# Two attention mixers on one core: V kept in one layout with drains of PE, nine exp tiles, another order of jobs on the shared PSUM bank, and a cubic for half of VectorE's exps

## The chip, the cores and the metric

The kernel runs on one core of one Trainium2 chip. The metric is the device time of one execution in microseconds. A core has TensorE (PE: matrix products), VectorE (DVE), ScalarE (ACT: here the exponentials), GpSimd (POOL) and SyncE (SP, which here only issues transfers). Each works through its own list of instructions in order and waits on semaphores for the others.

## The reference

```python
# x: [1, 2048, 512]; 32 heads of width 16; two attentions over the same x
# A: own q for each head, one k and one v shared by all heads
q = (x @ wq).reshape(B, S, H, Dh).transpose(0, 2, 1, 3); k = x @ wk; v = x @ wv
scores = einsum("bhqd,bkd->bhqk", q, k) * Dh ** -0.5
a = einsum("bhqk,bkd->bhqd", softmax(scores), v) -> [S, H*Dh] @ wo
# B: q, k and v for each head, from wqkv
b = the same with its own k and v, @ wo
g = sigmoid((x * gate_w).sum(-1, keepdims=True))
return g * a + (1 - g) * b
```

Weights and x are normal numbers of spread 0.05; A's wq and wk are multiplied by 8. There are 2 x 32 heads x 2048 x 2048 exponentials, 268 million. No row maximum is taken off in the kernel's fast path: the ranges of inputs, q and k are checked at the end, and a flag runs a general path (`_general`) if a limit is broken.

## The kernel before, in words

**Tiling.** Heads are handled in eight groups, in turn of A and of B (`groups`, L197: a0, b0, a1, b1, ...), eight heads each. A group has two halves of 1024 queries and for each half two phases of four heads: 32 phases (`phases`). A phase has 32 quads (`quads`, L200), each a block of 128 keys (`c`, 16 of them) with one of two pairings `w` of key halves and query blocks. A quad is two exp tiles (four heads): 2048 exp tiles of 128 x 1024 elements in all, keys along the partitions.

**Scores** (`products`, L616): eight matmuls of 64 rows by 32 columns fill a tile of two PSUM banks. Two such tiles alternate. ScalarE reads one with Exp into an SBUF tile of `prob_tiles` (L641, in `score`). There are six of these (`PROBS`).

**V products** (`values`, L669): PE multiplies the exps with V, in fp32, and sums over the 32 quads of a phase in PSUM, in the pair of banks `pair[0]`. The upper and the lower 64 key rows (`rows(i)`) sum into different banks. V has a column of ones, so the softmax's denominators come along. With `w` = 1 the key halves are exchanged, so V is held twice, in straight order and with its halves exchanged (`vA[0]`, `vA[1]`, `vB[0]`, `vB[1]`); the second is made by transfers (`swapped`, L213).

**The shared bank pair** `pair[1]` serves everything else on PE: the q, k and v projections (`project`, L422; 31 of 24 jobs each, L210), V's turning (`turned`), the output projections (`o_unit`, L496, six jobs each) and the scores of tiles whose exps VectorE does (`vector_job`, L799). Only one of these uses it at a time (`free["spare"]`, `current`).

**VectorE's exps** (`chain`, L827): a tile of scores goes through seven instructions: a conversion from PSUM (L843), mantissa (L847) and exponent (L851) by bit operations and four steps of Horner's scheme (L856), in six tiles `vec_tiles`. `pick` (L768) chooses a quad from the end of the present or the next phase, `vector_job` starts a chain if at most three of VectorE's tiles wait for their V product and little is left of the chain before.

**Other work.** After a phase the sums go to SBUF (L747), are rearranged by transfers (L565, SP's queue), divided (L572 to L581) and projected (`o_unit`); the results are scaled by the gate (L521) and added to the output in DRAM by GpSimd's queue (L531). q and k are split in two fp16 parts (L445, L448) and laid out for the scores by transfers of SP and POOL (`lay`, L404). GpSimd splits the weights (L226 to L228).

**What sets the order.** The program is written out while the kernel is made: a planner (`_Plan`) holds an estimated time for each engine. `pe_step` (L940) issues the next score tile as soon as its PSUM tile and an exp tile are free, and between two of them takes one job after another while it ends before the next exp is due. It asks, in this order, for V products of ScalarE's tiles (`mine`), for a job of the shared bank (`spare`) and for V products of VectorE's tiles (`other`); near a phase's end `other` comes ahead of `spare`. VectorE's instructions are chosen by rank and due time (`vector`, L107). Constants such as `EXP` (estimated distance of two exps, 904 ns) and `CHAIN` are the planner's.

## Time and profile before

| | |
|---|---|
| device time, median of 3 runs | 1826.82 us (1824.4 to 1826.92) |
| span of the profiled execution, first to last instruction | 1822.2 us |
| instructions | 95700 |
| busy: PE, VectorE, ScalarE, GpSimd | 96%, 73%, 98%, 17% |
| mean granted clock of TensorE | 0.996 |
| exp tiles on ScalarE, on VectorE | 1926, 122 |
| DMA moved | 109.39 MB, mean 60 GB/s |

The profiled execution has no time of its own beside its span; the median of the runs is 4.6 us above it. A row of the profile names the source line, engine, operation, output tile <- input tiles, shape and count; then busy time and mean duration of one; then the engine's idle time before such instructions and what ended it. Matmul rows overlap each other, so their busy time is not work; distances of starts are. A row of stretches gives begin:end and length in us, busy time and count of each engine, then the granted clock, the DMA share and GB/s.

### The profile page before, as it was taken

Reading aid. Unit: us, or ns where it says so; the run is one execution under the profiler, and the core shown is the slowest. Engines: PE = TensorE matmul, PEld = TensorE weight load, DVE = VectorE, ACT = ScalarE, POOL = GpSimd, SP = SyncE. Lnnn points to the kernel's source line nnn. Section 1 sums busy time; section 2 is a strip of 40 time slices with the busy share of each in tenths; the row PEclk is TensorE's granted clock in tenths of the full one; section 3 lists DMA queues with packets and bytes.
Section 4 is the critical chain, followed back from the end, with each engine's and each line's share of the span. In section 5 each row is a group of like instructions: output and inputs, shape, how many; then the busy total and the mean of one; then the engine's idle time right before and its main releaser. Section 6 shows DMA issues by size and latency. Waiting matters only on the chain.

```text
span 1822.2 us, 95700 instructions
## 1 busy us (share of the span) xinstructions
PE 1742.1 (96%) x44697; PEld 844.5 (46%) x44697; DVE 1332.0 (73%) x1507; ACT 1778.7 (98%) x1942; POOL 305.1 (17%) x367
## 2 busy tenths in 40 slices
PE   8999999999999999999999999999999999999896
PEld 5544444444444444444444444444444444444442
DVE  5277656779667597869767569796967676788994
ACT  5999999999999999999999999999999999999995
POOL 2212001202020131231102023133200111012000
PEclk9999999999999999999999999999999999999998
DMA  5121111323121142433212123342312122236111
GB/s 152 36 61 44 46 58 55 90 55 67 32 62 32 39 83 55 75 65 66 44 42 63 32 66 56 67 84 63 64 20 57 44 55 57 42 67 149 36 61 61
DMA packets 64883, 109.39 MB, mean 60 GB/s; under 512 B 14480, under 2 KB 22928, under 8 KB 64480
## 3 DMA queue, kind: packets, MB, share of 16 engines
q0 software_dynamic: 21504, 43.99, 13.6%
q1 hardware_dynamic: 39744, 56.99, 11.4%
q8 instruction: 351, 5.75, 1.3%
q10 hardware_dynamic: 3232, 2.23, 0.4%
q14 instruction: 52, 0.43, 0.1%
HBM read 14.75 MB, written 33.55 MB: 27 GB/s over the span
## 4 chain that ended last, share of the span: by engine, by line
ACT 86%; issue 8%; PE 4%; DVE 1%; DMA 1%; ACTq 0%; POOL 0%; DVEq 0%
ACT prob L641 85%; PE pair L682 1%; PE sc L627 1%; PE pair L301 0%; DVE vec L856 0%; PE pair L1173 0%; DMA prob<-in_A_wv_dram 0%; DVE xT L1295 0%; DMA vec<-in_A_x_dram 0%; DVE xT L515 0%; DMA Qa<-loqa 0%; PE pair L335 0%; DVE dT L572 0%; ACT early L641 0%; PE pair L210 0%
## 5 line engine op out<-in xcount | busy, mean ns | idle before, releaser
L641 ACT ACTIVATE prob<-sc 128x1024 f32<-128x1024 f32 x1905 | 1749.7, 1134 | 3.8 <-PE sc L627 3.2
L682 PE MATMUL pair<-prob,vA 64*32 64x512 f32 (+1 forms) x8048 | 510.4, 566 | 0.0
L682 PE MATMUL pair<-prob,vB 64*32 64x512 f32 (+1 forms) x8016 | 508.4, 569 | 0.0
L856 DVE SCALAR_TENSOR_TENSOR vec<-vec,vec 128x1024 f32<-128x1024 f32 x366 | 445.9, 1242 | 2.8
L627 PE MATMUL sc<-Qb,K 64*32 64x512 f16 x7632 | 395.9, 380 | 37.2 <-ACT prob L641 26.8
L627 PE MATMUL sc<-Qa,kA 64*32 64x512 f16 x7776 | 401.8, 380 | 21.7 <-ACT prob L641 11.6
L627 PEld LDWEIGHTS <-K 64*32 64x32 f16 x8192 | 201.2, 89 | 414.8 <-issue 375.1
L627 PEld LDWEIGHTS <-kA 64*32 64x32 f16 x8192 | 199.8, 89 | 390.2 <-issue 346.6
L843 DVE TENSOR_SCALAR vec<-pair 128x1024 int32<-128x1024 f32 x122 | 148.4, 1216 | 64.5 <-PE pair L627 64.4
L682 PEld LDWEIGHTS pair<-prob,vA 64*32 64x32 f32 x8048 | 155.3, 105 | 20.0 <-issue 1.4
L682 PEld LDWEIGHTS pair<-prob,vB 64*32 64x32 f32 x8016 | 153.5, 105 | 19.0 <-DVE raw L747 0.7
L856 DVE SCALAR_TENSOR_TENSOR vec<-vec 128x1024 f32<-128x1024 f32 x122 | 151.8, 1247 | 0.6
L531 POOL DMA_DIRECT2D out_dram<-sum x48 | 60.6, 1284 | 387.6 <-DVE sum L521 373.0
L572 DVE RECIPROCAL dT<-dT 128x256 f32<-128x256 f32 (+1 forms) x66 | 111.4, 1694 | 18.9 <-DMA dT<-raw 18.6
L747 DVE COPY raw<-pair 128x1024 f32<-128x1024 f32 x31 | 37.9, 1224 | 95.8 <-PE pair L682 95.2
L847 DVE TENSOR_SCALAR vec<-vec 128x1024 int32<-128x1024 int32 x122 | 84.1, 692 | 2.8 <-PE pair L682 1.3
L851 DVE TENSOR_SCALAR vec<-vec 128x1024 int32<-128x1024 int32 x122 | 84.5, 695 | 0.0
L521 DVE TENSOR_SCALAR sum<-pair,gate_up 128x512 f32<-128x512 f32 x112 | 78.6, 740 | 6.3 <-PE pair L210 6.0
L404 POOL DMA_DIRECT2D Qa<-hiqa x31 | 17.3, 558 | 305.6 <-DVE hiqa L445 284.5
L210 PEld LDWEIGHTS <-o 64*32 64x32 f16 x3072 | 50.1, 93 | 39.3 <-ACT o L578 8.1
L404 POOL DMA_DIRECT2D Qb<-hiqb x32 | 18.4, 574 | 293.3 <-DVE o L578 169.1
L210 PE MATMUL pair<-w16ob,o 64*32 64x512 f16 x1488 | 61.1, 384 | 6.0 <-ACT o L578 6.0
(160 smaller groups left out, 1182.7 us busy)
## 6 DMA issues: line engine op xcount, KB each, us to landing
out_dram<-sum POOLq DMA_DIRECT2D x48, 512.0 KB, 5.8
vB<-vB SPq DMA_DIRECT2D x16, 384.0 KB, 4.9
dT<-raw SPq DMA_DIRECT2D x32, 128.0 KB, 3.1
oT<-raw SPq DMA_DIRECT2D x32, 128.0 KB, 3.4
out_dram<-sum SPq DMA_DIRECT2D x8, 512.0 KB, 2.9
xT<-out_dram SPq DMA_DIRECT2D x16, 256.0 KB, 3.3
dT<-raw SPq DMA_DIRECT2D x62, 64.0 KB, 2.2
out_dram<-xT SPq DMA_DIRECT2D x12, 256.0 KB, 2.4
```

Source lines behind the costliest of these rows:

```text
L210: nc.tensor.matmul(outs[n : n + COLS, i], lhs[i][rows(i), n : n + COLS], rhs[i][rows(i)], start=start, stop=stop)
L521: nc.vector.tensor_scalar(state["sum"][:, e], pair[1][:, e], g, None, op0=ALU.mult)
L531: done = plan.on_pool([lambda: nc.gpsimd.dma_start(dst, state["sum"], accum_op=ALU.add)], t, 1300)
L572: nc.vector.reciprocal(d[:, c : c + cut], d[:, c : c + cut])
L627: nc.tensor.matmul(bank[a : a + COLS, hh], k[rows(hh), key : key + COLS], Q[src, gi, half, p][rows(hh), j * BLK : (j + 1) * BLK], start=Tr ...
L641: nc.scalar.activation(probs[u], sc, AF.Exp, scale=SCALE / (UP * UP))
L682: nc.tensor.matmul(pair[0][32 * k : 32 * k + 32, i, cols], v[rows(i)], probs[2 * m + k // 2][rows(i), hh, cols], start=first, stop=last)
L747: nc.vector.tensor_copy(state["raw"], full)
L843: nc.vector.tensor_scalar(tile("p").bitcast(I32), pair[1], SCALE / (UP * UP) / math.log(2) * 2.0 ** 23, None, op0=ALU.mult)
L847: nc.vector.tensor_scalar(tiles["m"].bitcast(I32), tiles["p"].bitcast(I32), 0x7FFFFF, 125 << 23, op0=ALU.bitwise_and, op1=ALU.bitwise_or)
L851: nc.vector.tensor_scalar(tiles["w"].bitcast(I32), tiles["p"].bitcast(I32), 0x7F800000, 0x40000000 | LEAD, op0=ALU.bitwise_and, op1=ALU.bi ...
L856: nc.vector.scalar_tensor_tensor(p, m if i == 3 else p, VEC[i], m if i else w, op0=ALU.add, op1=ALU.mult)
```

## The change

V is held once. The scores keep the keys in place and exchange the query blocks instead (`j = a // ROWS ^ w`), so with `w` = 1 the upper and lower rows of a V product write the other bank of `pair[0]`. A phase's quads come in runs of the same `w` (8, 16 and 8 long), and where the V products change `w` within three score tiles, PE executes a drain first. The memory of the second V gives three more exp tiles. While more than `LEFT` (near a phase's end `LEFT_END`) exp tiles are free, the order of asking is `spare`, `mine`, `other`. VectorE's tiles of B take three instructions, a cubic in factored form; to bound B's scores the check of q_b takes sums of magnitudes over a head by a matmul (`magnitudes`) in place of a plain maximum. `pick` goes by runs, with less lead (`CHAIN` 16000); a tile of VectorE's is summed when its `w` suits the present run or free tiles are few. Transfers that lay out q and k are issued once the tiles they overwrite are no longer needed (`behind`); V's turning waits for the old group's V products.

```diff
-EXP, EXP_ENDS, EXP_AFTER = 904, 1136, 456
+EXP, EXP_ENDS, EXP_AFTER = 916, 1148, 456
-PROBS, VECS = 6, 6
+PROBS, VECS = 9, 6
+LEFT, LEFT_END = 2, 4
+DRAINED, KEPT, SPARED = 180, 2, 2
...
-    vA = [cst.tile([P, NT, DH, 2], F32, name=f"vA{w}") for w in range(2)]
-    vB = [cst.tile([P, NT, 4, 3, DH], F32, name=f"vB{w}") for w in range(2)]
+    vA = cst.tile([P, NT, DH, 2], F32, name="vA")
+    vB = cst.tile([P, NT, 4, 3, DH], F32, name="vB")
...
-    quads = [(ph, c, w) for ph in range(len(phases)) for c in range(NT) for w in range(2)]
+    ORDER = [(c, w ^ h) for h in range(2) for w in range(2) for c in range(8 * h, 8 * h + 8)]
+    FIRST = [(c, 0) for c in (0, 4, 1, 2, 3, 5, 6, 7)] + ORDER[8:]
+    quads = [(ph, c, w) for ph in range(len(phases)) for c, w in (ORDER if ph else FIRST)]
+    runs = [[] for _ in range(3 * len(phases))]
+    for m in range(len(quads)):
+        runs[m // 32 * 3 + (m % 32 >= 8) + (m % 32 >= 24)].append(m)
...
-            swapped(vA[1][:, ts], vA[0][:, ts], queue)
...
+    waiting = []
+    def behind(m, fn):
+        waiting.append((m, fn))
+    def reads():
+        for m, fn in list(waiting):
+            if at[0] >= m and not (half_vec and half_vec[0] // 2 < m):
+                waiting.remove((m, fn))
+                fn(plan.pe)
...
-                plan.vec(lambda: absmax(kind, 2 * gi + half, hilo[0], AX.XY), 1130, 4, end, due=end + 8000)
+                if kind == "q_b":
+                    plan.vec(lambda: magnitudes(2 * gi + half, hilo[0]), 330, 2, end, due=end + 4000, room=lambda: free_vecs)
+                else:
+                    plan.vec(lambda: absmax(kind, 2 * gi + half, hilo[0], AX.XY), 1130, 4, end, due=end + 8000)
...
-                    put(hilo, end)
+                    s = 2 * (2 * gi + (src == "b")) + half
+                    behind(64 * (s - 1) if part == "q" else 256 * gi, lambda t: put(hilo, max(t, end)))
...
+    def magnitudes(n, hi):
+        tile = free_vecs.popleft()
+        mag = tile.rearrange("p a q -> p (a q)")[:, :BLK]
+        nc.vector.tensor_scalar(mag.bitcast(I32), hi.rearrange("p e t -> p (e t)").bitcast(I32), 0x7FFF7FFF, None, op0=ALU.bitwise_and)
+        mag = mag.bitcast(F16).rearrange("p (e t) -> p e t", e=2)
+        def job():
+            for i in range(2):
+                for e in range(2):
+                    nc.tensor.matmul(pair[1][COLS * e : COLS * (e + 1), i], heads16[rows(i)], mag[rows(i), e], start=True, stop=True)
+            free_vecs.append(tile)
+        def finish(t):
+            def top():
+                nc.vector.tensor_reduce(stats[: 2 * COLS, KINDS.index("q_b"), n : n + 1], pair[1][: 2 * COLS], axis=AX.XY, op=ALU.max)
...
-                done = plan.on_sp([lambda: swapped(vB[1][:, ts], vB[0][:, ts], nc.sync)], end, 2 * ISSUE_SP)
...
-        units.append(_Unit(jobs, finish, lambda now: True, lambda: 0, f"turn{gi}{half}"))
+        units.append(_Unit(jobs, finish, lambda now: pv_at[0] >= 8 * gi, lambda: 0, f"turn{gi}{half}"))
...
-                key = c * P + (a + ROWS * w) % P
-                j = a // ROWS
+                key = c * P + a
+                j = a // ROWS ^ w
...
+        if turns(m):
+            nc.tensor.drain()
+            summing[w ^ 1] = -3
...
-                nc.tensor.matmul(pair[0][32 * k : 32 * k + 32, i, cols], v[rows(i)], probs[2 * m + k // 2][rows(i), hh, cols],
+                nc.tensor.matmul(pair[0][32 * k : 32 * k + 32, i ^ w, cols], v[rows(i)], probs[2 * m + k // 2][rows(i), hh, cols],
                                  start=first, stop=last)
+        summing[w] = len(plan.starts)
...
+    def suits(m):
+        rest = [x for x in range(32 * pv_at[0], 32 * pv_at[0] + 32) if x not in vector and x not in added]
+        return not rest or quads[rest[0]][2] == quads[m][2] or len(free_vecs) < SPARED
+    def turns(m):
+        begun = put_in[0] + len(going) > (m in [x for x, _ in going.values()])
+        return begun and summing.get(quads[m][2] ^ 1, -3) + 3 > len(plan.starts)
...
-            can = [m for m, t in pending[pv_at[0]] if (m not in vector) == mine and max(t, v_time(m)) <= now]
+            can = [m for m, t in pending[pv_at[0]] if (m not in vector) == mine and max(t, v_time(m)) <= now and (mine or suits(m))]
...
-        ns = HALF * wide * 2 // BLK
+        ns = HALF * wide * 2 // BLK + (DRAINED if turns(m) else 0)
...
-        need = CHAIN + plan.backlog(3)
...
+        need, left = CHAIN + plan.backlog(3), 0
+        for r in range(at[0] // 32 * 3, min(at[0] // 32 * 3 + 6, len(runs))):
+            found = [m for m in runs[r] if m not in vector and m >= at[0]]
+            left += 2 * len(found)
+            if left * EXP > need and len(found) > KEPT and found[-1] >= at[0] + 2:
+                break
...
+        if source(quads[u // 2][0]) == "b":
+            def first():
+                nc.vector.tensor_scalar(tile("p"), pair[1], CUBE[0] * SCALE / (UP * UP), CUBE[1], op0=ALU.mult, op1=ALU.add)
+            def second():
+                nc.vector.scalar_tensor_tensor(tile("w"), tiles["p"], CUBE[2], tiles["p"], op0=ALU.add, op1=ALU.mult)
+            def third():
+                nc.vector.scalar_tensor_tensor(p, w, CUBE[3], p, op0=ALU.add, op1=ALU.mult)
...
-    CHAIN, MOST, EARLY = 24000, 18, 12
+    CHAIN, EARLY = 16000, 12
...
-        first = (spare, mine, other) if begins and len(free_probs) > 1 else (mine, other, spare) if ending else (mine, spare, other)
+        first = (spare, mine, other) if begins and len(free_probs) > 1 or len(free_probs) > (LEFT_END if ending else LEFT) else (mine, other, spare) if ending else (mine, spare, other)
...
-        nc.vector.tensor_scalar(lim[:, r + k : r + k + 2], highest[:, ix("q_a") : ix("q_b") + 1],
-                                S_MAX / (DH * SCALE), None, op0=ALU.is_le)
+        for src, most in (("q_a", S_MAX / (DH * SCALE)), ("q_b", B_MAX / SCALE)):
...
```

71 lines of the change are left out of this document (44 added, 27 removed).

## The prediction

> **What bounds the kernel now.** I read the page first (busy time, then the chain that ended last), then the rows of the exp line, then stretches of the span.
>
> ```profile
> span 1822.2 us, 95700 instructions
> PE 1742.1 (96%) x44697; PEld 844.5 (46%) x44697; DVE 1332.0 (73%) x1507; ACT 1778.7 (98%) x1942; POOL 305.1 (17%) x367
> ACT 86%; issue 8%; PE 4%; DVE 1%; DMA 1%; ACTq 0%; POOL 0%; DVEq 0%
> L641 ACT ACTIVATE prob<-sc x1905: 1017/1145/1182, 28.1 to 1799.7; 128x1024 f32<-128x1024 f32 x191
> L641 ACT ACTIVATE vec<-sc x10: 1019/1026/1096, 33.7 to 62.9; 128x1024 f32<-128x1024 f32 x10
> L641 ACT ACTIVATE early<-sc x8: 1017/1031/1107, 38.4 to 63.8; 128x1024 f32<-128x1024 f32 x8
> L641 ACT ACTIVATE vB<-sc x3: 1024/1024/1030, 47.5 to 51.9; 128x1024 f32<-128x1024 f32 x3
> 929.74 103.82 ACT L641 ACTIVATE prob<-sc 128x1024 f32<-128x1024 f32 x113
> ```
>
> ScalarE is busy 98% and carries the chain. It does 1905 + 10 + 8 + 3 = 1926 exp tiles, first start 28.1, last 1799.7: 1771.6 us for 1925 distances, 0.920 each. The last row is an undisturbed stretch of 113: with the last one's own 1.15 taken off, (103.82 - 1.15) / 112 = 0.917 us from start to start. So only 1771.6 - 1925 x 0.917 = 6 us are gaps; 28.1 lie before the first exp and 22.5 behind the last start. The time is the number of exps on ScalarE times 0.917 plus about 57. An exp tile moved to VectorE is worth 0.917 us, if PE and VectorE keep up.
>
> [...]
>
> VectorE takes 122 of the 2048 tiles (122 x the five rows below). Is it full, and is PE?
>
> ```profile
> L843 DVE TENSOR_SCALAR vec<-pair 128x1024 int32<-128x1024 f32 x122 | 148.4, 1216 | 64.5 <-PE pair L627 64.4
> L847 DVE TENSOR_SCALAR vec<-vec 128x1024 int32<-128x1024 int32 x122 | 84.1, 692 | 2.8 <-PE pair L682 1.3
> L851 DVE TENSOR_SCALAR vec<-vec 128x1024 int32<-128x1024 int32 x122 | 84.5, 695 | 0.0
> L856 DVE SCALAR_TENSOR_TENSOR vec<-vec 128x1024 f32<-128x1024 f32 x122 | 151.8, 1247 | 0.6
> L856 DVE SCALAR_TENSOR_TENSOR vec<-vec,vec 128x1024 f32<-128x1024 f32 x366 | 445.9, 1242 | 2.8
> 258.00:480.00 222.00, 213.66 (x5463) 101.84 (x5455) 156.77 (x172) 221.84 (x243) 39.23 (x47) 1.00 0.26 64
> 480.00:703.00 223.00, 217.04 (x5632) 104.69 (x5617) 165.05 (x182) 222.77 (x244) 37.21 (x46) 1.00 0.23 53
> 703.00:921.00 218.00, 209.79 (x5392) 101.00 (x5391) 169.03 (x185) 217.84 (x239) 48.16 (x48) 1.00 0.32 61
> 1585.00:1802.00 217.00, 203.66 (x5072) 95.22 (x5056) 179.09 (x211) 215.27 (x235) 19.84 (x22) 1.00 0.30 69
> ```
>
> The last four rows are stretches of one head group each (groups alternate A, B): B's first, A's second, B's second, B's last; behind the length stand busy PE, PE loads, VectorE, ScalarE, GpSimd. VectorE is idle 40 to 65 us in each. The page's 96% for PE overstates it, since pipelined matmuls overlap; so I price PE by distances of starts.
>
> ```profile
> 784.86 0.41 PE L627 MATMUL sc<-Qb,K 64*32 64x512 f16 x8
> 785.08 0.63 PE L210 MATMUL pair<-w16oa,o 64*32 64x512 f16 x16
> 785.63 0.41 PE L627 MATMUL sc<-Qb,K 64*32 64x512 f16 x8
> 785.84 1.05 PE L682 MATMUL pair<-prob,vB 64*32 64x512 f32 x16
> 786.70 0.41 PE L627 MATMUL sc<-Qb,K 64*32 64x512 f16 x8
> ```
>
> A tile's scores take 0.22 (784.86 to 785.08), a product job of eight matmuls 0.22 (0.63 - 0.41), the V product of a pair of tiles (a quad) 0.86 (785.84 to 786.70). Two ScalarE slots last 1.84 and hold 0.22 + 0.43 + 0.22 + 0.86 = 1.73: 94% full, 0.11 idle. The product and exp counts by stage (same four stretches, L210 then L843):
>
> ```profile
> 258.00:480.00 222.00, 45.67 (x1152) 18.70 (x1152) 1.00 0.26 64
> 480.00:703.00 223.00, 49.08 (x1264) 20.48 (x1264) 1.00 0.23 53
> 703.00:921.00 218.00, 41.10 (x1048) 16.82 (x1040) 1.00 0.32 61
> 1585.00:1802.00 217.00, 30.68 (x768) 12.40 (x760) 1.00 0.30 69
> 258.00:480.00 222.00, 17.01 (x14) 1.00 0.26 64
> 480.00:703.00 223.00, 19.48 (x16) 1.00 0.23 53
> 703.00:921.00 218.00, 19.43 (x16) 1.00 0.32 61
> 1585.00:1802.00 217.00, 21.98 (x18) 1.00 0.30 69
> ```
>
> A group has 256 tiles, so 256 x 0.22 + 128 x 0.86 = 166 us of scores and V products, and products of 1152/8 x 0.22 = 32, 35, 29, 21. PE's need is 198, 201, 195, 187 of 222, 223, 218, 217: 86 to 90%. PE has some 20 us left per group, VectorE 40 to 65.
>
> Why does VectorE take no more? Its scores and all projections share one PSUM bank, `pair[1]`:
>
> ```profile
> L210 PE MATMUL pair<-xT,w16vb x192: 376/376/376, 989.1 to 1009.5; 64*32 64x512 f16 x192
> DVE hikb L445 <- PE pair L210: 75.1, 8, 15.9
> DVE hivb L445 <- PE pair L210: 72.4, 8, 15.5
> DVE hiqb L445 <- PE pair L210: 42.6, 8, 15.3
> DVE hiqa L445 <- PE pair L210: 36.9, 7, 7.3
> ```
>
> One projection, 24 jobs of 0.22 or 5.3 us of PE, is spread at two jobs per two slots over 20.4 us, and 31 of them hold the bank a third of the time. Meanwhile VectorE runs dry: 227 us of its idle time ended with a projection's last product.
>
> **The change, part by part.**
>
> Cubic for B's exps. Five kinds of operation in seven instructions, 1.216 + 0.692 + 0.695 + 1.247 + 3 x 1.242 = 7.58 us, become one from PSUM and two in SBUF: 1.216 + 2 x 1.242 = 3.70. In B's second group VectorE has 169 - 16 x 7.58 = 48 us of other work, so it could do (0.9 x 209 - 48) / 3.70 = 38 tiles instead of 16. A's stay at 7.58. For this, q_b's check costs a mask and a job of the shared bank more: eight times about 0.36 (half of the 692 row) and 0.22 of PE, 5 us over the span, hidden in VectorE's idle time.
>
> Shared banks' products first, nine tiles. While more than two tiles are free, jobs of the bank go ahead of V products: a slot then holds three jobs rather than one, until the spare tiles are used up. A projection shrinks from 20.4 to about 12 us (estimate: some four slots of three jobs, the rest at one or two). No PE work is saved; the V products put off return as a debt, and PE's room decides.
>
> V held once. Sixteen transfers of vB (the row below) and four of vA go from SP's and POOL's queues, off the path: V is ready most of a group before its use, which hides them. Without that cover the price would be the 4.9 us of landing.
>
> ```profile
> vB<-vB SPq DMA_DIRECT2D x16, 384.0 KB, 4.9
> K<-lokb SPq DMA_DIRECT2D x32, 64.0 KB, 3.2
> ```
>
> Delayed stores of Q and K (`behind`): sixteen DMAs per projection, alternately on SP and POOL, are issued later, but still 64 quads (over 110 us) before use for Q, 128 for K; landing takes 3.2. V's turn waits until the old group's V products are done; behind it wait only the hi/lo buffers, so the next projection. Cost nothing; cover gone, a projection starts some us late with 110 us to spare. The waits move out of the in-order queues into the program's order.
>
> Drains. Two changes of row halves per phase make 64; a quad of VectorE's out of the run's order adds up to two, so with about 91 quads of VectorE 64 to 246. I take 128, 16 a group. No drain is in this trace. What it exposes is the tail behind the last start of a group: 0.41 - 0.22 = 0.19; with nothing overlapped, all 0.41. I take 0.2, nearest the tail, 3 us per group; ends 64 x 0.19 = 12 to 246 x 0.41 = 101 us of PE in all. Queued behind a drain are the next V product and then the scores that the next exp waits for; in the full pattern they have about 0.1 to 0.2 us of slack, so I put nothing on ScalarE. [...]
>
> The sum. How full can PE get? 94% is the present full pattern; nine tiles let a job fall where the 0.11 was idle. I take 95%; ends 92% (about now) and 98%.
> - B's second and third: (195 + 3) / 0.95 = 208 us, 227 slots, 29 tiles for VectorE instead of 16: +12.6 each (VectorE 75% busy).
> - B's first: 201 / 0.95 = 212, 231 slots, 25 instead of 14: +11.
> - B's last: 190 / 0.95 = 200, 218 slots, 38; VectorE at 90%, with 179 - 18 x 7.58 = 43 of other work, does 37 instead of 18: +19.
> - A's second to fourth: 204 / 0.95 = 215, 234 slots would allow 22; VectorE, with 165 - 16 x 7.58 = 44 of other work and still seven instructions a tile, at 87% does 19 instead of 16: +3 each. A's first: none.
>
> That is +55 in B, +9 in A: 64 tiles, 59 us. Gaps, start and end stay at 57: span 1763.5, against 1822.2. The median of the runs shown, 1826.82, is 4.6 above this span (the record gives the profiled execution no other time). **Predicted: 1768 us.** [...]
>
> **Rivals.**
> 1. PE packs no better (92%): B gains 5, 5, 4, 12, A nothing: 26 tiles, 24 us, 1803. For it: every full stretch shows the same 0.11 idle. Against: B's last group is only 86% full.
> 2. Tiles are held, not computed faster: at most four of VectorE's may wait for their V product, which now comes last in order and only when its half suits. With one batch per phase, 32 x 4 = 128 tiles: 6 us, 1821. Against: the stretches are 8 and 16 quads long, so there are two chances a phase, and lack of tiles overrides the fit.
> 3. Both engines pack better (PE 98%, VectorE 92%): B +20, +20, +18, +19, A +4 each: 93 tiles, 85 us, 1742.
> 4. Slower: each drain stalls ScalarE, because the scores behind it come later than their slack. With 246 drains at the whole 0.41, 101 us of idle exps: 1827 - 59 + 101 = 1869. It decides from 59 / 246 = 0.24 us of stall per drain. For it: scores run only just ahead, since both score banks are in use. Against: the tail row is 0.19, and the order gives a slot with a drain less work.
> 5. The change doesn't do what it says: if q times k of B passed the new limit, the general path would run behind the fast one and the time would multiply. With weights and x of spread 0.05, scores are hundredths; under 1%.
>
> **How the numbers follow.** Main 0.58, PE at 92% 0.17, held tiles 0.10, better packing 0.07, slower 0.08. The main case's own range is 1750 to 1790. The range of 8 in 10 reaches past case 1 and to case 3: 1740 to 1815. A measurement tells 0.2% (3.7 us; the three runs spread 2.5) from no change. Faster: 0.58 + 0.17 + 0.07 + half of the held case 0.05 = 0.87; same 0.05; slower 0.08.
>
> **What would show it.** Right: some 1862 exps on ScalarE, 0.917 apart in undisturbed stretches; about 186 chains on VectorE, two thirds in B at three instructions; projections of 10 to 14 us; PE's need about 95% of each group. Wrong: idle time of ScalarE behind score matmuls near drains beyond the present 6 us (rival 4); counts near 130 with VectorE idle and the bank free (rival 2); projections still 20 us long. If the distance of exps moves from 0.917 by 0.01, 19 us change hands that no step above has.

## The result and the profile after

The change makes the kernel slower: 1869.56 us (median of 4 runs, 1864.53 to 1875.38) against 1825.61 for the kernel before in the same runs, a ratio of 1.0247 (95% interval 1.0233 to 1.0260). 1768 was predicted, and "faster". In the kernel after, the exps stand on L689, the scores on L675, the V products on L734, the jobs of the shared bank on L220, the drain on L724, VectorE's cubic on L946, L949 and L953, and its long chain from L908 on.

The page of the kernel after, its span and busy time:

```profile
span 1867.5 us, 115071 instructions
PE 1767.6 (95%) x54505; PEld 1039.6 (56%) x54505; DVE 1214.0 (65%) x1348; ACT 1763.4 (94%) x1908; POOL 280.7 (15%) x363
```

VectorE does less than before (65% against 73%) and ScalarE is busy 94% instead of 98%, while PE executes 54505 + 54505 = 109,010 matmuls and weight loads instead of 89,394. VectorE and ScalarE have less to do, PE more, and the span is 45.3 us longer: something makes them wait. First the exps (rows of the exp line; the last two numbers of a time are first and last start):

```profile
L689 ACT ACTIVATE prob<-sc x1875: 1014/1081/1194, 27.3 to 1844.2; 128x1024 f32<-128x1024 f32 x188
L689 ACT ACTIVATE vec<-sc x9: 1024/1031/1077, 37.2 to 65.9; 128x1024 f32<-128x1024 f32 x9
```

With five into `early` and three into `vB` these are 1892 exps, 34 fewer than before. I took all 1891 distances of their starts. Those below 930 ns have a mean of 909.8 ns (before: 914.9), and what the longer ones have above this mean I call **excess**. Then the 45.3 us are: 34 exps fewer, -31.1; a distance shorter by 5.1 ns, -9.6 (why it is shorter, no run here shows); excess 96.6 instead of 10.4, +86.2; ahead of the first and behind the last start 50.6 as before, 0. So the exps saved were worth what I said, there were half as many, and 86 us of waiting came that no term of the sum had.

Whom does ScalarE wait for, and whom does that one wait for? The waits of the kernel after (total us, times, longest us), and ahead of them the row of before that answers to the second:

```profile
PEld pair L682 <- issue: 2.7, 8, 0.7
```

```profile
ACT prob L689 <- PE sc L675: 62.5, 70, 3.2
PEld pair L734 <- issue: 97.6, 164, 3.4
PE pair L734 <- issue: 24.2, 24, 2.9
PEld pair L734 <- DVE raw L811: 8.7, 11, 1.9
```

ScalarE waits for score matmuls, and PE, ahead of V products, for "issue": nothing that the profile shows, neither a semaphore nor a transfer. (A larger row of this kind, weight loads ahead of scores, stands in both kernels and is not the loss: 721.7 us before, 357.8 after, some 0.27 each.) The last row, a wait for VectorE's copy of a phase's sums, had 0.7 us before. One place of such an "issue", PE's timeline of the kernel after from 758 us on:

```profile
761.31 0.43 PE L675 MATMUL sc<-Qb,K 64*32 64x512 f16 x8
...
762.06 0.41 PE L675 MATMUL sc<-Qb,K 64*32 64x512 f16 x8
762.27 0.62 PE L734 MATMUL pair<-prob,vB 64*32 64x256 f32 x14
765.78 0.40 PE L734 MATMUL pair<-prob,vB 64*32 64x256 f32 x1 [2.89 <-issue]
```

PE is in the middle of a V product of 16 matmuls: 14 are through, the last two have nothing to wait for, and one of them starts three microseconds later. Between the first and the last exp PE has 26 pauses of over 1 us, and before it had none.

**Where they stand.** I numbered all of PE's instructions in the trace in their order (matmuls, loads, drains, semaphore instructions). 21 of the 26 stand ahead of an instruction whose number leaves 193 when divided by 256, and no other remainder comes twice; the other five wait for VectorE (the copy L811 of a phase's sums, or the low part of q, L468). PE's program comes in blocks of 256 instructions, as the queue that carries it shows (packets, MB, share):

```profile
q8 instruction: 428, 7.01, 1.6%
```

109,010 / 256 = 426, and the 7.01 MB in 428 packets are 16.4 KB each. I read a pause at the end of a block as a block that hasn't arrived yet.

The trace has the times of these packets too. In the pause above one landed at 764.42, and PE went on at 765.78, 1.36 us later. With blocks and packets counted from the first, PE goes on behind each of the 21 pauses 1.22 to 1.54 us after the landing of the packet whose number is one below that of the block end. Where a block ends without a gap, that packet landed 1.9 us ahead (median; 3.2 in the kernel before), and at none of 423 block ends less than 1.18. So it is its block that PE waits for in these pauses, and nowhere does it start on one sooner than 1.18 us after the landing.

**Why PE has more instructions.** The planner cuts a V product in two halves of 256 columns where the room until the next score doesn't hold the whole. A half takes as many matmuls and loads as a whole: 904 products cut in two are 28,928 instructions more in b_halves, 32 each. The rows of the V products of before (min/median/max ns):

```profile
L682 PE MATMUL pair<-prob,vA x8048: 373/589/614, 35.3 to 1584.3; 64*32 64x512 f32 x175, 64*32 64x256 f32 x22
L682 PE MATMUL pair<-prob,vB x8016: 373/589/613, 258.6 to 1801.4; 64*32 64x512 f32 x179, 64*32 64x256 f32 x17
```

and of after:

```profile
L734 PE MATMUL pair<-prob,vA x13896: 372/376/1057, 35.9 to 1632.6; 64*32 64x256 f32 x175, 64*32 64x512 f32 x24
L734 PE MATMUL pair<-prob,vB x11616: 372/376/614, 268.6 to 1845.9; 64*32 64x256 f32 x144, 64*32 64x512 f32 x53
```

The usual V product was 512 columns wide and is now 256: with the jobs of the shared bank first, the room that is left is rarely enough for a whole one. The rate of instructions follows. Stretches of 10 us of the kernel after (behind the length busy time and count of PE, its loads, VectorE, ScalarE, GpSimd; then granted clock, DMA share, GB/s):

```profile
740.00:750.00 10.00, 9.92 (x320) 5.60 (x312) 5.62 (x12) 10.00 (x12) 0.87 (x1) 1.00 0.37 57
750.00:760.00 10.00, 8.58 (x273) 4.84 (x257) 1.92 (x3) 8.63 (x10) 3.65 (x3) 1.00 0.74 109
760.00:770.00 10.00, 7.11 (x239) 4.38 (x244) 1.41 (x2) 6.76 (x9) 0.00 (x0) 1.00 0.33 54
```

320 + 312 instructions in 10 us are 63 per us, a block in 4.05 us; the kernel before has 49 per us over its span, a block in 5.2. In the first row the blocks come in time, in the other two they don't. What differs is the DMA share ahead of the two pauses, that of 756.94 and that of 762.52; the 4 us ahead of each (the share adds up the times of the packets and can be over 1: 1.10 in the first):

```profile
752.94:756.95 4.01, 4.01 (x150) 2.43 (x135) 0.52 (x1) 4.01 (x6) 0.00 (x0) 1.00 1.10 185
758.52:762.53 4.01, 3.79 (x128) 2.38 (x127) 0.00 (x0) 3.38 (x4) 0.82 (x1) 1.00 0.73 97
```

For 416 block ends of the trace I took the DMA share of the 4 us ahead: where it was below 0.6, none of 348 had a pause over 1 us; from 0.6 on, 20 of 68 had one. The program's queue is one of those whose packets the page counts on the 16 DMA engines, beside the kernel's transfers: 1.6% of their time for the program, 13.2%, 9.6% and 0.4% for the three queues of transfers.

### The profile page after: what moved, and what is told of

It is laid out like the page before. It is cut to its first block, busy times and chain, and to the rows that moved or that the text cites. A ratio compares the mean times of both kernels' runs of the same rounds, so it can differ in the third digit from the quotient of the medians.

```text
span 1867.5 us, 115071 instructions
## 1 busy us (share of the span) xinstructions
PE 1767.6 (95%) x54505; PEld 1039.6 (56%) x54505; DVE 1214.0 (65%) x1348; ACT 1763.4 (94%) x1908; POOL 280.7 (15%) x363
## 2 busy tenths in 40 slices
DMA packets 63454, 104.08 MB, mean 56 GB/s; under 512 B 14160, under 2 KB 22480, under 8 KB 62976
## 3 DMA queue, kind: packets, MB, share of 16 engines
q0 software_dynamic: 21440, 43.86, 13.2%
q8 instruction: 428, 7.01, 1.6%
## 5 line engine op out<-in xcount | busy, mean ns | idle before, releaser
L689 ACT ACTIVATE prob<-sc 128x1024 f32<-128x1024 f32 x1875 | 1738.0, 1085 | 64.9 <-PE sc L675 62.5
L734 PE MATMUL pair<-prob,vA 64*32 64x256 f32 (+1 forms) x13896 | 603.5, 398 | 23.3 <-issue 15.3
L734 PE MATMUL pair<-prob,vB 64*32 64x256 f32 (+1 forms) x11616 | 554.7, 434 | 13.6 <-issue 7.0
L675 PE MATMUL sc<-Qa,kA 64*32 64x512 f16 x7760 | 436.1, 381 | 10.1 <-ACT prob L689 4.3
L675 PE MATMUL sc<-Qb,K 64*32 64x512 f16 x7376 | 406.7, 380 | 20.7 <-ACT prob L689 10.9
L734 PEld LDWEIGHTS pair<-prob,vA 64*32 64x32 f32 x13896 | 286.9, 106 | 116.3 <-issue 49.2
L675 PEld LDWEIGHTS <-K 64*32 64x32 f16 x8192 | 194.2, 90 | 273.7 <-issue 218.1
L675 PEld LDWEIGHTS <-kA 64*32 64x32 f16 x8192 | 189.7, 90 | 204.3 <-issue 139.8
L734 PEld LDWEIGHTS pair<-prob,vB 64*32 64x32 f32 x11616 | 236.2, 106 | 79.9 <-issue 32.0
L921 DVE SCALAR_TENSOR_TENSOR vec<-vec,vec 128x1024 f32<-128x1024 f32 x162 | 197.2, 1226 | 2.0
L946 DVE TENSOR_SCALAR vec<-pair 128x1024 f32<-128x1024 f32 x102 | 123.2, 1208 | 46.9 <-PE pair L675 44.4
L953 DVE SCALAR_TENSOR_TENSOR vec<-vec,vec 128x1024 f32<-128x1024 f32 x102 | 124.9, 1229 | 0.8
L949 DVE SCALAR_TENSOR_TENSOR vec<-vec 128x1024 f32<-128x1024 f32 x102 | 123.8, 1223 | 0.8
L908 DVE TENSOR_SCALAR vec<-pair 128x1024 int32<-128x1024 f32 x54 | 66.0, 1222 | 74.7 <-PE pair L675 72.6
L220 PEld LDWEIGHTS <-o 64*32 64x32 f16 x3072 | 56.5, 93 | 40.0 <-ACT o L626 8.8
L811 DVE COPY raw<-pair 128x1024 f32<-128x1024 f32 x31 | 37.8, 1220 | 52.5 <-PE pair L734 52.5
L734 PE MATMUL pair<-vec,vB 64*32 64x256 f32 (+1 forms) x1568 | 66.4, 386 | 3.1 <-issue 1.9
L921 DVE SCALAR_TENSOR_TENSOR vec<-vec 128x1024 f32<-128x1024 f32 x54 | 66.4, 1230 | 1.0
```

Source lines behind the costliest of these rows:

```text
L220: nc.tensor.matmul(outs[n : n + COLS, i], lhs[i][rows(i), n : n + COLS], rhs[i][rows(i)], start=start, stop=stop)
L675: nc.tensor.matmul(bank[a : a + COLS, hh], k[rows(hh), key : key + COLS], Q[src, gi, half, p][rows(hh), j * BLK : (j + 1) * BLK], start=Tr ...
L689: nc.scalar.activation(probs[u], sc, AF.Exp, scale=SCALE / (UP * UP))
L734: nc.tensor.matmul(pair[0][32 * k : 32 * k + 32, i ^ w, cols], v[rows(i)], probs[2 * m + k // 2][rows(i), hh, cols], start=first, stop=last)
L908: nc.vector.tensor_scalar(tile("p").bitcast(I32), pair[1], SCALE / (UP * UP) / math.log(2) * 2.0 ** 23, None, op0=ALU.mult)
L921: nc.vector.scalar_tensor_tensor(p, m if i == 3 else p, VEC[i], m if i else w, op0=ALU.add, op1=ALU.mult)
```

## The experiments

**Theory 1**, formed from the trace of after: PE can't be supplied with that many instructions; the halves are the cause. **Theory 2** is the rival from the prediction: the drains stall ScalarE. A third reading is that the new order of jobs alone is late. The first three runs put one part alone into the kernel before; the fourth takes halves out of the kernel after by one constant, and drains and exps move along with it. The table has all runs, each with its ratio to runs of the kernel before made beside it (medians 1824.7 to 1825.6); the last three columns split the excess of the exps by what lies in the interval or shortly ahead of it: a gap of over 0.2 us in PE's starts at the end of a block, a drain (or both, shown behind the plus sign), or neither.

| kernel | us | ratio to before, 95% | exps | PE instructions | block end | drain + both | neither |
|---|---|---|---|---|---|---|---|
| before | 1825.61 | 1 | 1926 | 89,394 | 3.5 | 0 | 6.9 |
| after | 1869.56 | 1.0247, 1.0233 to 1.0260 | 1892 | 109,010 | 46.4 | 12.7 + 9.2 | 28.2 |
| b_halves | 1879.84 | 1.0282, 1.0257 to 1.0308 | 1926 | 118,322 | 58.7 | 0 | 15.8 |
| b_drains | 1846.48 | 1.0113, 1.0095 to 1.0131 | 1926 | 89,394 | 2.8 | 30.1 + 4.9 | 5.3 |
| b_cubic | 1817.10 | 0.9947, 0.9928 to 0.9966 | 1912 | 89,650 | 7.3 | 0 | 12.3 |
| a_tight574 | 1824.40 | 0.9995, 0.9985 to 1.0004 | 1874 | 96,850 | 20.8 | 16.4 + 1.9 | 28.0 |
| b_quarters | 2762.43 | one run | 1926 | 183,858 | 921.8 | 0 | 26.2 |
| b_prodhalves | 1870.53 | 1.0238, 1.0216 to 1.0261 | 1926 | 107,442 | 47.0 | 0 | 15.8 |
| a_left35 | 1833.26 | 1.0050, 1.0033 to 1.0067 | 1908 | 97,650 | 17.3 | 7.3 + 1.3 | 15.0 |
| a_nocubic | 1886.18 | 1.0330, 1.0313 to 1.0348 | 1916 | 107,346 | 34.7 | 14.8 + 11.0 | 33.8 |
| a_drain2 | 1881.78 | 1.0324, 1.0296 to 1.0352 | 1892 | 109,010 | 50.9 | 16.6 + 13.5 | 25.8 |
| a_left35_fewdrains | 1833.27 | 1.0047, 1.0033 to 1.0060 | 1902 | 98,322 | 19.8 | 1.0 + 0 | 21.0 |
| b_copies | 1853.15 | 1.0153, 1.0119 to 1.0188 | 1926 | 89,394 | 31.4 | 0 | 9.7 |
| b_halves_copies | 2019.84 | 1.1079, 1.1058 to 1.1101 | 1926 | 118,322 | 184.2 | 0 | 23.2 |

### Halves alone, in the kernel before

```diff
-        wide = BLK if n == 0 and plan.scant() and room + TIGHT - SLACK >= 2 * HALF else BLK // 2
+        wide = BLK // 2
```

> The kernel before with one edit: every V product is cut in two halves of 256 columns, where before 904 of the 1024 went at full width. Same arithmetic, same order, same 1926 exps on ScalarE, no drain; PE gets some 904 x 32 = 28900 instructions more (from 89400 to about 118300). Theory 1 (PE is fed too slowly: it stops once it needs more than some 64 instructions a us, as in the 4 us before the long stops of the changed kernel): 118300 / 64 = 1848 us for the instructions alone and with head and tail 1860 to 1910, with many stops of PE over 1 us that wait for nothing. Theory 2 (the drains cost the time) and theory 3 (PE's arithmetic is full): within 5 us of before, 1821 to 1831, since the columns streamed are the same and there is no drain.

Measured: +54.7 us by the medians (51.5 by the ratio) with nothing else changed: no drains, no cubic, the old order, V twice. From its page and its waits:

```profile
span 1878.6 us, 124628 instructions
PE 1774.7 (94%) x59161; PEld 1097.6 (58%) x59161; DVE 1333.4 (71%) x1507; ACT 1794.1 (96%) x1942; POOL 300.3 (16%) x367
```

```profile
PEld pair L682 <- issue: 36.3, 62, 2.0
ACT prob L641 <- PE sc L627: 40.6, 65, 2.3
```

The same two rows as in the kernel after stand up. All 19 pauses over 1 us between the first and the last exp lie at the same remainder, 193.

### Drains alone, in the kernel before

```diff
+        if put_in[0] in (8, 16, 24) and cols.start == 0:
+            nc.tensor.drain()
         for k in range(4):
```

> The kernel before with 96 drains of PE added, ahead of the V products of the 9th, 17th and 25th quad of each phase; nothing else. Theory 1: PE has room for them, at most +8 us (1826 to 1834), for 96 x the tail of 0.19 us is 18 us of PE work of which most is idle time now. Theory 2 (drains stall ScalarE): the 0.41 us of a whole group or more each, +40 us, 1865 or above.

Measured: +21.3 us, between the two expectations. The kernel has 91 of the 96 drains, 0.23 us each: at the other five places a second half comes, and the edit asks for a first. The drain's row and the wait (PEldq is the queue of PE's instructions):

```profile
L676 PEldq DRAIN  x91: 435/470/955, 54.4 to 1809.9; - x91
```

```profile
PEld pair L684 <- issue: 41.9, 98, 0.6
```

A drain holds PE for 0.47 us, and about half of it reaches ScalarE, so a drain isn't free, but 91 of them aren't the 44 us either. The excess at drains is larger than the cost, 30.1 to 35.0 us: the distance of the other exps is 909.7 ns instead of 914.9, and that gives 10 us back. No pause over 1 us came with them.

### The cubic alone, in the kernel before

```diff
+        if groups[phases[quads[u // 2][0]][0]][0] == "b":
+            # first, second, third: one tensor_scalar from PSUM, two scalar_tensor_tensor, as in the change
...
+            return
         a = plan.vec(convert, 1130, 1, t + TO_VEC, (), spared, room=lambda: free_vecs)
```

The check of q_b isn't widened with it, so nothing bounds B's scores for the cubic; the condition under which the last output tiles are loaded early is eased as in the change.

> The kernel before with only the cubic for VectorE's tiles of B (three instructions instead of seven), and with the outputs of the last group let be loaded while that group's own projections wait, as the changed kernel does; V twice, six tiles, the old order and the old range check stay (the check does not bound B's scores for the cubic). The order has 1912 exps on ScalarE instead of 1926, so 14 x 0.917 = 13 us less: 1813, if the cubic's gain is real and PE can follow. If the gain of a freed VectorE is eaten elsewhere (a rival: PE or the shared bank gives no more), 1822 to 1830.

Measured: 1817.10 us, below both kernels, by half a percent of before (ratio 0.9947). A row of VectorE:

```profile
L882 DVE TENSOR_SCALAR vec<-pair 128x1024 f32<-128x1024 f32 x90 | 109.6, 1218 | 47.3 <-PE pair L628 47.3
```

90 tiles by the cubic and 46 by the long chain, 136 instead of 122: 14 exps fewer, 12.8 us, less 9.2 us of new excess in the profiled execution (whose 1819.47 us is the slowest of its four runs). VectorE was 73% busy before and is 61% busy now, and takes only 14 tiles more: with the chain less than half as long for B, something other than VectorE's time limits most of the number. Which, the run doesn't show.

### Fewer halves, in the kernel after

`TIGHT` is how far past its due time a whole V product may end.

```diff
-SLACK, TIGHT, URGENT = 404, 404, 300
+SLACK, TIGHT, URGENT = 404, 574, 300
```

> The changed kernel with one constant changed: a V product of full width may run 170 ns past the time at which the next scores are due (TIGHT 574 instead of 404). The order then has 673 V products at full width and 702 in halves, instead of 293 and 1462: about 12000 PE instructions fewer (near 96900), 77 drains instead of 96 and 1874 exps on ScalarE instead of 1892. Theory 1: the stops go; 28 + 1874 x 0.91 + 23 and 10 to 30 us of gaps: 1770 to 1795. Theory 2: 77 of 96 drains remain, so about 80% of the excess stays: 1835 to 1855. Theory 3 (PE's arithmetic is full): more exps go to VectorE, PE's arithmetic is the same, so no better than 1860.

Measured: 1824.40 (10 runs), 45 us faster than the kernel after by one number of the planner, but 29 to 54 above what I expected. From its page:

```profile
span 1821.9 us, 102877 instructions
PE 1734.3 (95%) x48425; PEld 927.6 (51%) x48425; DVE 1300.3 (71%) x1426; ACT 1750.6 (96%) x1890; POOL 287.1 (16%) x363
```

12,160 instructions fewer, excess at block ends 46 to 21 us, and 18 exps fewer (16 us), I take it since PE has time for more of VectorE's scores. What I had missed is the rest, 46 us of excess at drains (18) and in 241 small gaps (28), 0.1 us at a time, in which neither a block end nor a drain lies. That the order of jobs itself comes late there is my reading; no run shows it.

### How many instructions per us PE can get

```diff
-        wide = BLK if n == 0 and plan.scant() and room + TIGHT - SLACK >= 2 * HALF else BLK // 2
+        wide = BLK // 4
```

> The kernel before with every V product cut in four pieces of 128 columns: same columns streamed, same 1926 exps on ScalarE, no drain, PE instructions from 89400 to about 183900. Theory 1 (PE is fed at some 64 instructions a us at most): 183900 / 64 = 2870 us, and the mean rate over the span tells the ceiling. Rival (short matmuls just cost a fixed time more each on PE itself): b_halves added 28900 instructions and 55 us, 1.9 ns each, so 94500 more would add 180 us: about 2005.

Measured: 2762.43 us, 183,858 instructions in 2760.7 us, 66.6 per us, a little more than the 64 that I had expected. From its page:

```profile
span 2760.7 us, 190171 instructions
PE 1922.1 (70%) x91929; PEld 1537.9 (56%) x91929; DVE 1343.3 (49%) x1507; ACT 1871.7 (68%) x1942; POOL 287.2 (10%) x367
...
q8 instruction: 720, 11.80, 1.8%
...
L641 ACT ACTIVATE prob<-sc 128x1024 f32<-128x1024 f32 x1905 | 1841.5, 1024 | 840.0 <-PE sc L627 833.7
```

No engine is busy throughout, and the kernel runs at the pace of the blocks: 183,858 / 256 = 718, and 720 packets. 603 of its 605 pauses over 1 us between the first and the last exp stand at the remainder 193, and nine in ten of these end 1.23 to 1.55 us after their packet landed. Outside the pauses over 1 us PE starts 102 instructions per us, so it is not the starting of an instruction that limits it.

### More instructions of another kind

Here the V products stay and the fp16 products of the shared bank are cut in two, so that 18,048 instructions come in other places.

```diff
-                nc.tensor.matmul(outs[n : n + COLS, i], lhs[i][rows(i), n : n + COLS], rhs[i][rows(i)],
-                                 start=start, stop=stop)
+                for c in range(0, BLK, BLK // 2):
+                    cols = slice(c, c + BLK // 2)
+                    nc.tensor.matmul(outs[n : n + COLS, i, cols], lhs[i][rows(i), n : n + COLS], rhs[i][rows(i)][:, cols],
+                                     start=start and c == 0, stop=stop and c > 0)
```

> The kernel before with the products of the projections (the jobs of the shared bank, fp16) cut in two halves of 256 columns each; V products stay as they were. PE instructions from 89400 to about 107400, as many as in the changed kernel, but in other places and in another type. Theory 1: during a projection two slots then need 32 + 64 + 32 = 128 instructions in 1.83 us, 70 a us, above the ceiling of 64, so each of 31 projections of 22 us runs some 9% late, and the output projections in part: +40 to +65 us, 1865 to 1890, with stops of PE. Rival (it is something of fp32 V products in halves): 1821 to 1831.

Measured: 1870.53, as expected by theory 1, with 47 us of excess at block ends. So the loss needs neither V nor its banks nor its fp32; what the two edits share is more and narrower instructions of PE, and b_quarters and the packets say that the number is what counts.

### Less of the new order, in the kernel after

```diff
-LEFT, LEFT_END = 2, 4
+LEFT, LEFT_END = 3, 5
```

> The changed kernel with jobs of the shared bank put first only while more than 3 (near a phase's end 5) exp tiles are free instead of 2 and 4. The order then has 648 V products at full width and 752 in halves (before the edit 293 and 1462), 82 drains, 1908 exps on ScalarE. Theory 1 with the price of a drain from b_drains (0.22 us): 28 + 1908 x 0.91 + 18 for drains + 10 to 25 of stops + 23 = 1815 to 1832. Drains as the main cause: 82 of 96 remain, so above 1850.

Measured: 1833.26, a microsecond above the expected range. Shared jobs go first only while more than three tiles are free; more V products find room as a whole (97,650 instructions), and the excess falls at block ends (46 to 17 us), near drains and in the small gaps. 16 exps more go back to ScalarE (15 us). Halves come from asking the shared bank first.

### Without the cubic, in the kernel after

```diff
-        if source(quads[u // 2][0]) == "b":
+        if False:
```

> The changed kernel without the cubic: VectorE's tiles of B take the seven instructions again; all else stays (the order puts 1916 exps on ScalarE instead of 1892, 345 V products at full width and 1358 in halves, 93 drains). If the cubic gives inside the change what it gave alone (0.917 us for each exp moved), 24 x 0.92 = +22 us: 1885 to 1897. If its gain is lost in a PE that is fed too slowly, the time hardly moves: 1860 to 1875.

Measured: 1886.18, in the expected range: 24 tiles go back from VectorE to ScalarE, and the cubic is worth about 15 us within the change by the ratios (1.0330 - 1.0247 = 0.0083 of 1825), 17.6 by the medians, each against its own runs of before, somewhat less than the 22 of its exps.

### Each drain twice, in the kernel after

```diff
         if turns(m):
             nc.tensor.drain()
+            nc.tensor.drain()
```

> The changed kernel with each of its 96 drains doubled (two in a row), order and all else the same. If a drain costs because PE has to run empty and fill again, the second finds it empty: 0 to +5 us, 1865 to 1875. If each drain costs the 0.22 us of b_drains whatever stands ahead of it (a fixed cost of the instruction), +21 us: 1887 to 1895.

Measured: 1881.78, 12 us above the kernel after, between the two expectations. The drain's row in the kernel after, and the rows of the first and the second of each pair in this one:

```profile
L724 PEldq DRAIN  x96: 457/578/1470, 56.4 to 1834.4; - x96
```

```profile
L724 PEldq DRAIN  x96: 432/616/1462, 56.2 to 1845.1; - x96
...
L725 PEldq DRAIN  x96: 13/13/248, 57.2 to 1845.7; - x96
```

A second drain finds PE empty and takes 13 ns, so the edit doesn't double what I meant to double. The excess grows by 10 us, 8 of them at drains, more than the 1.2 us of the added rows, and why is open. For the price of a drain the run says little.

### Fewer drains

```diff
-LEFT, LEFT_END = 2, 4
-DRAINED, KEPT, SPARED = 180, 2, 2
+LEFT, LEFT_END = 3, 5
+DRAINED, KEPT, SPARED = 400, 2, 0
```

> The kernel of a_left35 (jobs of the shared bank first only above 3 or 5 free tiles) with a V product of VectorE's tiles never let through out of its run (SPARED 0) and a drain reckoned at 400 ns instead of 180 by the order: 40 drains instead of 82, 1902 exps on ScalarE instead of 1908, about as many V products in halves (some 21 more jobs of 32 instructions), and an end some 6 us longer by the order. At 0.22 us a drain: -9 for drains, -5 for exps, +10 for the later end and gaps that the order itself leaves: 1824 to 1832 against a_left35's 1833. If the drains hold most of what is left of the excess (41 us there), below 1820; if drains cost nothing, 1833 to 1840.

Measured: 1833.27 (9 runs), the same as with 82 drains. At the 40 drains left lies 1 us of excess instead of 8.6, and there are six exps fewer (5.5 us); but the distance is longer (912.3 ns against 910.4, 3.6 us), 8.5 us more of excess lie at block ends and in small gaps, and 3.1 us more ahead of the first and behind the last exp. The order of the tiles moved with the drains, so this run doesn't settle what a drain costs inside the change.

### The other factor: transfers

The DMA share ahead of the pauses was a correlation. These two runs add idle copies of 256 KB to the kernel before and to the one with halves, whose output doesn't depend on them: 124 MB or 473 copies, since the places that fall on VectorE's tiles are skipped.

```diff
+    apart = ctx.enter_context(tc.tile_pool(name="apart", bufs=1, space=bass.MemoryType.DRAM)).tile([64, P, D], F32, name="apart")
+
     def score(u):
+        if u % 4 == 0 and 64 <= u:
+            nc.sync.dma_start(apart[u // 4 % 64], x[u // 4 % NT * P :][:P, :])
         sc = ps_s.tile([P, ACT, BLK], F32, tag="sc", name=f"sc{u}")
```

> The kernel before with 496 idle copies of 256 KB from DRAM to DRAM, one at every fourth score tile, on SP's queue: nothing uses what they write. They roughly double what the DMA engines move. Refill theory: PE's instructions come in blocks of 256 over the DMA engines; before uses up a block in about 5.2 us (1822 us / 351), slow enough that a refill delayed by other transfers is still in time: 1825 to 1840 us, at most a few stops of PE over 1 us. Rival (transfers cost time by themselves, through SP's queue or late operands): as much added here as in the same edit on the halves, with ScalarE or PE waiting for DMA rows. Rival (transfers have nothing to do with the stops): nothing added in either.

> The kernel with every V product in two halves, and with the same 496 idle copies. It uses up a block of 256 instructions in about 4.05 us (1879 us / 464). In its trace without the copies the stops over 1 us stand where the DMA engines were over 0.6 busy in the 4 us ahead (16 of 71 such block ends, 2 of 381 others). Refill theory: with the copies some 150 to 250 block ends fall into such stretches instead of 71, each worth 0.4 to 0.6 us of ScalarE: 1880 + 35 to 100, so 1915 to 1980 us, with 40 or more stops over 1 us, all at the same place of a block of 256 instructions. Rival (stops are set by the number of instructions alone): 1875 to 1890 us, about 20 stops.

Measured: +28 us in the kernel before, 13 above the expected range, and +140 in the one with halves, 40 above it. Both are in the direction of the refill theory, and larger. Waits of the kernel with halves and copies:

```profile
ACT prob L645 <- PE sc L627: 160.2, 159, 4.3
PEld pair L686 <- issue: 108.6, 121, 3.4
```

All 76 pauses over 1 us between the first and the last exp stand at the remainder 193, and so do all 10 in the kernel before with copies, which without them has none. The pauses by the DMA share of the 4 us ahead of a block end (from some 50 us on, so that one pause of the kernel after and one of the halves are not in it):

| kernel | share below 0.6: ends, with a pause over 1 us | from 0.6: ends, with a pause over 1 us |
|---|---|---|
| before | 287, 0 | 52, 0 |
| before with copies | 209, 1 | 130, 9 |
| after | 348, 0 | 68, 20 |
| halves | 381, 2 | 71, 16 |
| halves with copies | 296, 4 | 156, 72 |

The same copies cost 28 us at 49 instructions per us and 140 at 63. Transfers that cost time by themselves would have cost as much in both, and stops set by the number of instructions alone would not have moved. A block that is used up in 5.2 us mostly arrived in time, even beside other transfers (9 pauses at 130 ends with a share from 0.6 on); of those that are used up in some 4 us, 72 of 156 didn't when the DMA engines were that busy.

## Why the prediction was wrong, point by point

**What bounds the kernel: right.** ScalarE's exps, 0.91 apart, set the time of the kernel before; each tile taken from it is worth that, if PE keeps up. In b_cubic 14 tiles fewer are 12.8 us, of which 8 reach the median; in the kernel after PE doesn't keep up, and 34 tiles fewer bring nothing. (The 1145 ns in the row of the exps are of exps that run back to back; the 11 exps of before that start on an idle ScalarE take 1025 ns, and 1023 is the median in b_quarters.)

**"How full can PE get? I take 95%": the step that failed.** I added the columns that PE streams (0.22 a score tile, 0.86 a V product of two tiles) and left the number of instructions out. "V products put off return as a debt, and PE's room decides" is true, but they return in halves, since three shared jobs in a slot leave no room for 0.86. A half has half the columns and all the instructions. PE's program grew by 22%, past what arrives in time beside the transfers, and 43 us of new excess at block ends came of it (46.4 - 3.5), and part of the 9 us that drains and block ends share. The source could have told me: the planner of before carries constants, `RATE` = 0.062 instructions per ns with a `STORE` of 200, and asks before each whole product whether PE's instructions are `scant` (with `SCANT` = 201 above the store the answer is always yes). I read past them because the profile of before shows next to nothing of such a wait ahead of V products: the row quoted above has 2.7 us.

**Drains: "0.2 on PE, nothing on ScalarE": too low.** The number was near (96 against 128), the duration on PE was 0.47 to 0.58. On ScalarE each cost 0.23 us where nothing else was changed; in the kernel after 13 to 22 us of excess lie at drains. ("No drain is in this trace" overlooked three at the ends of the trace of before, of 8 ns each on an idle PE; they would have told nothing.)

**Nine tiles and shared products first: a projection from 20.4 to 12 us: wrong.** From the start of the first product to that of the last the 31 projections take 19.0 us (median) instead of 20.4. One of them, rows of the kernel after in a stretch of 75 us:

```profile
L220 PE MATMUL pair<-xT,w16vb x192: 373/376/376, 1006.6 to 1026.1; 64*32 64x512 f16 x192
```

In the first 2 us of a projection 5.3 jobs start instead of 3.0, on the mean, and from 6 us on about two in 2 us as before: I take it that the free tiles are used up at once and the order falls back to the old one. So VectorE still runs dry while projections hold the bank:

```profile
DVE hiqa L465 <- PE pair L220: 81.4, 6, 25.7
DVE hiqb L465 <- PE pair L220: 72.8, 7, 26.5
DVE hivb L465 <- PE pair L220: 68.8, 7, 20.2
DVE hikb L465 <- PE pair L220: 63.9, 8, 11.2
```

287 us instead of 227.

**The cubic: 3.70 us a tile: right; the number of tiles: too high.** The rows of after:

```profile
L946 DVE TENSOR_SCALAR vec<-pair 128x1024 f32<-128x1024 f32 x102 | 123.2, 1208 | 46.9 <-PE pair L675 44.4
L949 DVE SCALAR_TENSOR_TENSOR vec<-vec 128x1024 f32<-128x1024 f32 x102 | 123.8, 1223 | 0.8
L953 DVE SCALAR_TENSOR_TENSOR vec<-vec,vec 128x1024 f32<-128x1024 f32 x102 | 124.9, 1229 | 0.8
L908 DVE TENSOR_SCALAR vec<-pair 128x1024 int32<-128x1024 f32 x54 | 66.0, 1222 | 74.7 <-PE pair L675 72.6
```

1.208 + 1.223 + 1.229 = 3.66. But 102 tiles of B and 54 of A, 156, were taken rather than 186. 30 exps at 0.915 are 27 us of the miss.

**V once and the later stores at nothing: nothing speaks against it.** PE waits 1.9 us in all for a transfer into `Qa`, as before, and for none into `Qb` or `K`. What is worth adding is that 109.39 MB moved became 104.08: V's copies were transfers. That fewer of them help PE's program arrive, no run shows by itself.

**The sum.** 1763.5 was predicted for the span, 1867.5 was measured. The 104 us are 27.6 for tiles not taken and 86.2 of excess, less 9.6 for the shorter distance. The excess grew by 42.9 at block ends, 12.7 at drains, 9.2 at both, and 21.3 in gaps with neither.

**The rivals.** The fourth gave 1869, the time that was measured, with a chance of 0.08, and for another reason: it put 101 us on 246 drains at 0.41, and the 96 drains bring 13 to 22. The first (1803) and the second (1821) named limits that are there, PE's room and tiles not taken, without the loss. (The third's 93 tiles count +4 in four groups of A, where the main sum leaves A's first out; with three they are 89, and 1745 instead of 1742.) None had the number of instructions. Of "what would show it", idle time of ScalarE behind scores was named as the sign of wrong, but it was to lie near drains; about half of it lies at block ends.

**What stays open.** Of the 21 us in gaps with neither, some 5.5 lie in four intervals where PE waits for VectorE's copy of a phase's sums (L811, the last row of the waits), a wait that the prediction left out. The rest I put down to the new order of jobs, since these gaps, 28.2 in all, fall to 15.0 with `LEFT` = 3 and stay at 28 with `TIGHT` = 574, but no run shows it by itself. The excess at drains inside the change lies between 12.7 us (intervals with a drain alone) and 21.9 (those with a block end too), 0.13 to 0.23 each (in b_drains 0.33 to 0.38 by the same count, with a net cost of 0.23); neither the doubled nor the fewer drains narrow it. Nine tiles with V held twice were not tried. The best kernel of these runs is the one of before with the cubic, 1817.10, still without B's bound on the scores.

## What to carry to other kernels

Count an engine's instructions as well as its work: where PE runs at some 50 to 60 instructions per us, as here, a matmul of half the columns is not half the price (904 V products in halves cost 54.7 us in b_halves), and a schedule that fills gaps with smaller pieces can starve PE of its own program. Pauses that wait for nothing, always at the same remainder of 256 instructions (21 of 26 in the kernel after, 603 of 605 in b_quarters), are the sign, and the packets of the program's queue, landing 1.2 to 1.5 us ahead of the end of each of the 21, are the proof. Fewer and wider instructions are a remedy (12,160 fewer and 45 us in a_tight574); transfers moved away from the dense stretches might be another, which was not tried here. And numbers in a planner that no row of the profile explains (here a rate and a store) may be limits that someone met before: ask of each change whether it comes back to them.

## What the runs showed of the hardware

- PE's instructions come in blocks of 256 over the DMA engines (428 packets for 109,010 matmuls and loads in the kernel after, 720 for 183,858 in b_quarters). The highest mean rate over a span was 66.6 per us (b_quarters). At 49 per us PE had no pause over 1 us with the DMA queues at 60 GB/s (the kernel before) and 10 with them at 126 (b_copies). PE starts on a late block 1.2 to 1.6 us after its packet has landed (21 pauses of the kernel after, nine in ten of 603 in b_quarters).
- A drain of PE has a duration of 0.47 us (median, b_drains) to 0.58 (the kernel after), and cost ScalarE's chain 0.23 in b_drains; a second one right behind it takes 13 ns (a_drain2).
- Behind two of the 26 pauses of the kernel after the granted clock was lower. The 3 us behind one of these two, a pause of 2.7 us from start to start, and behind another of 3.3 us:

```profile
1135.82:1138.82 3.00, 3.00 (x56) 1.79 (x63) 0.95 (x1) 1.03 (x2) 0.01 (x1) 0.63 0.89 122
765.78:768.78 3.00, 3.00 (x105) 1.94 (x107) 0.18 (x1) 1.70 (x2) 0.00 (x0) 1.00 0.02 5
```

The granted clock was 0.63 behind the shorter, with 56 matmuls in the 3 us, and 1.00 behind the longer, with 105; behind 24 of 26 pauses it was 1.00. What lowers it, these runs don't show. At two of 26 it is a small part of the loss.
